# A two-pass channel-attention kernel: the first 26 rows of the second pass are loaded into the stream slots behind the last loads of the first

## The chip, the core and the metric

The kernel runs on one core of a Trainium2 chip. The metric is device time in microseconds (us) of one execution; the figure for a kernel is the median of its runs. TensorE is called PE in the profile's rows, VectorE DVE, ScalarE ACT, SyncE SP, GpSimd POOL. All loads and stores of the large tensor are issued by SP, in one order, onto one queue that 16 DMA engines work off.

## The reference

`x` has the shape (1, 384, 384, 384) in bfloat16, `w1d` holds one weight. The weight's window has length one, so the 1-D convolution over channels is a product:

```python
g  = jnp.einsum("bhwc->bc", x) / (H * W)      # mean over all 147456 positions
s  = sigmoid(g * w1d[0])
return x * s[:, None, None, :]
```

Every output element needs `s`, and `s` needs every input element. `x` is 113.25 MB; it does not fit into the core's on-chip memory, so a part of it has to be read twice.

## The kernel before, in words

**Rows.** The 147456 positions are 1152 rows for each of the 128 partitions. "A row" below is 128 partitions x 384 channels in bfloat16, which is 98304 bytes, and all buffers are counted in rows. One on-chip tensor, `arena` (L175), holds 275 of them; the names below are row numbers in it.

**Pass one** loads all 1152 rows, and PE adds each into `bank0` by a product with a matrix of ones (`sum_rows`, L224). Three kinds of rows pass through.

- *Streamed* rows (`stream`, L328): loaded, summed, overwritten. They are loaded again in pass two. There are `N_STREAM` = 785 of them.
- *Folded* rows (`fold`, L271): four rows are packed into the place of three by DVE and ACT, using exponent bits that are the same in the data; 296 rows are kept so, some of them in PSUM banks. They are unpacked in pass two by `unfold` (L446).
- *Raw* rows (`c_raw`, `N_RAW` = 71): the last 71 rows of pass one, which simply stay where they were loaded: 39 in area `A` (three slots of 13, L367, which streamed rows have used before), 8 each in `V`, `U`, `Y` and `T`. `U`, `V`, `Y` and `T` serve `fold` as scratch until then. `take_raw` (L414) writes their loads into the order: the three slots of `A`, then `V`, `U`, `Y`, `T` (5 and 3 rows).

**Between the passes** ACT computes the scale `s_bf` from `bank0` (L421). It waits for the last matmul; DVE's first multiplication waits for it; SP's first store waits for that.

**Pass two** multiplies each row by `s_bf` on DVE (`scale`, L428, whose instruction the profile has on L432) and stores it (`store`, L438, on L442). Rows that are free after their store are refilled with streamed rows, which are multiplied and stored in turn. Held and reloaded rows together make 1152 stores and 785 loads.

**What sets the order of pass two** is a planner that runs while the program is built (L539 to L717). It steps a clock from the moment the scale is there, keeps a list of what the queue has still to move (`moves`, with assumed costs per row and per transfer) and decides at each step what DVE does next (a multiplication from `landed`, or a piece of a folded pair), when a store is sent, and when a free run of rows is refilled (L695 to L706). What comes out is a fixed order of instructions on DVE and on SP. `Flow` (L21) adds the semaphore waits; SP takes its list strictly in order, so a load that waits for a store to land holds every transfer behind it.

The refill rule before is this:

```python
if n >= BIG or n == N_STREAM - todo or (ahead < LOW and n >= 8) or ahead < LAST:
```

Here `n` is the longest free run, `ahead` the planned backlog of the queue in us, `BIG` is 32 rows, `LOW` 9.0 and `LAST` 4.0.

Of the kernel before, what the change touches and what calls it, by code (L numbers as in the profile page):

```python
# [127 lines left out]
def kernel(  # L128
# [28 lines left out]
        areas.append((base, 3 * q))  # L157
        base += 3 * q
    RAW = {}
    for name, n in (("U", 8), ("V", 8), ("A", 39), ("Y", 8), ("T", 8)):  # L160
        RAW[name] = (base, n)
        base += n
    ROWS = base
    N_RAW = sum(n for _, n in RAW.values())
    U, V, A, Y, T = (RAW[n][0] for n in "UVAYT")

    BANKED = len(QS)
    PS = 3 * Q_BANKS
# [24 lines left out]
    def view(t, r0, n):  # L193
        return t[r0 * P : (r0 + n) * P, :].rearrange("(p r) c -> p r c", r=n)

    def rows(lo, n):
        return [("a", r) for r in range(lo, lo + n)]
# [3 lines left out]

    N_STREAM = RPP - N_RAW - sum(4 * q for q in QS)
    r = N_STREAM
    c_group = []
    for q in QS:
        c_group.append((r, 4 * q))
        r += 4 * q
    c_raw = (r, N_RAW)
    assert r + N_RAW == RPP

# [3 lines left out]
    def load(chunk, a, lo=0, hi=None):  # L214

        r0, n = chunk
        hi = n if hi is None else hi
        fl.add(
            "SP",
            lambda: nc.sync.dma_start(out=arena[:, a : a + hi - lo, :], in_=view(xf, r0, n)[:, lo:hi, :]),  # L220
            writes=rows(a, hi - lo), dma=True,
        )

    def sum_rows(a, n):  # L224
        def emit(i, first, last):
            return nc.tensor.matmul(acc, lhsT=ones[:], rhs=arena[:, i, :], start=first, stop=last)  # L226

        for i in range(a, a + n):
            first, last = summed[0] == 0, summed[0] == RPP - 1
            fl.add(  # L230
                "PE", lambda i=i, f=first, l=last: emit(i, f, l),
                reads=[("a", i), "ones"], writes=["bank0"],
            )
            summed[0] += 1
# [132 lines left out]
    SLOTS = [(A + i, 13) for i in range(0, 39, 13)]  # L367
# [3 lines left out]
    S1, S2, S3 = ([slot] for slot in SLOTS)  # L371
    B3, B4, AA = ([area] for area in (areas[3], areas[4], (A, 39)))

    def halves(area):
        a, n = area
        return [(a, n // 2), (a + n // 2, n - n // 2)]
# [4 lines left out]
        ([], B3), ([], B4),  # L381
        ([], B3), ([], AA),
        ([], halves(areas[4])), ([], S1 + S2 + S3),
        (S1, S2, S3 + S1), (S2, S3, S1 + S2 + S3),
    ]
    between = sum(n for b in BETWEEN[1:] for where in b for _, n in where)
    at = 0
    for g, q in enumerate(QS[:BANKED]):
        for lo in range(0, q, 2 * PIECE):
            n = min(2 * PIECE, q - lo)  # L390
# [19 lines left out]
            at += 1  # L410
    assert streamed[0] == N_STREAM

    def take_raw(a, n):
        load(c_raw, a, a - U, a - U + n)  # L414
        sum_rows(a, n)

    for a, n in SLOTS + [(V, 8), (U, 8), (Y, 8), (T, 5), (T + 5, 3)]:
        take_raw(a, n)
    assert summed[0] == RPP

    fl.add(  # L421
# [61 lines left out]
    def TT(n):  # L483
        return 0.15 + 0.2 * n
# [54 lines left out]
    ROW, PER_LOAD, PER_STORE = 0.2267, 0.112, 0.061  # L539
    LAT, SEEN, DT = 2.0, 1.5, 0.05  # L540
    PENDING, MERGE = 24.0, 12.0
    BIG, CAP, PART, LOW, LAST = 32, 48, 16, 9.0, 4.0
    BANKS_AT = 2
    now = dve_at = 0.0
    moves, waiting, over, acts = deque(), deque(), deque(), deque()
    landed = deque()
    idle = [False] * ROWS
    todo = 0
# [18 lines left out]
    def send(chunk, a, lo, hi, then, known=None):  # L567

        waiting.append((dve_at, hi - lo, then, chunk, a, lo, [] if known is None else known))

    def backlog():
        return sum(e[1] for e in moves) + ROW * sum(e[1] for e in waiting)

    def split(n, m):
        k = -(-n // m)
        cuts = [n * i // k for i in range(k + 1)]
        return list(zip(cuts, cuts[1:]))
# [12 lines left out]
        return f  # L590


    landed.append((c_raw, Y, Y - U, 4, False))
    landed.append((c_raw, Y + 4, Y - U + 4, 4, True))
    landed.append((c_raw, T, T - U, 8, True))
    landed.append((c_raw, U, 0, 8, True))
    for e, n in ((0, 8), (8, 13), (21, 13), (34, 13)):
        landed.append((c_raw, V + e, 8 + e, n, True))

    HALVES = (T, U)  # L600
    half = [True, True]
# [11 lines left out]
    def start_pair():  # L613

        nonlocal pair, bank_at
        if not line or needed or not half[pair % 2]:
            return False
        g, lo, n = line[0]
        if g == BANKED and (bank_at is None or now < bank_at[1]):
            return False  # L620
        line.popleft()
        h = pair % 2
        at = HALVES[h]
        half[h] = False
        pair += 1
        a = bank_at[0] if g == BANKED else areas[g][0]
        a += 3 * lo
        mine = [k for k in of_group(g) if lo <= pieces[k][1] < lo + n]

        def w_done():  # L630
            nonlocal out_rows
            out_rows += n
            release(a, 3 * n)

        def u_done():
            half[h] = True

        for k in mine:
            e = pieces[k][1] - lo
            fields, three, fourth = unfold(k, a + 3 * e, at + e)  # L640
            turns.extend((fields + (None,), three + (None,), fourth + (None,)))
        f, t, _ = turns[-2]
        turns[-2] = (f, t, lambda: send(c_group[g], a, 3 * lo, 3 * (lo + n), w_done, written))
        f, t, _ = turns[-1]
        turns[-1] = (f, t, lambda: send(c_group[g], at, 3 * QS[g] + lo, 3 * QS[g] + lo + n, u_done, written))
        return True

    while True:

        if dve_at <= now:  # L650
            ahead = backlog()
            can = bool(turns)
            if not can and (ahead >= PENDING or not landed):
                can = start_pair()
                if can and not asked:
                    verdict()
                    asked = True
            if landed and (ahead < PENDING or not can):
                chunk, a, lo, n, end = landed.popleft()
                scale(a, n)  # L660
                dve_at = now + TT(n)
                since = (a, lo) if since is None else since
                if end or ahead < MERGE:
                    b, first = since
                    send(chunk, b, first, lo + n, stored(b, lo + n - first))
                    since = None
            elif can:
                f, t, then = turns.popleft()
                f()
                dve_at = now + t  # L670
                if then:
                    then()
        while waiting and waiting[0][0] <= now:
            _, n, then, chunk, a, lo, known = waiting.popleft()
            known.append(store(chunk, a, lo, lo + n))
            moves.append([now + LAT, n * ROW + PER_STORE, then])
        if out_rows == total and not checked and all(half):
            checked = True
            fl.add("POOL", again, reads=["odd_i", "s_bf"], writes=rows(Y, N_OVER), after=written)
        while over and over[0][0] <= now:  # L680
            over.popleft()[1]()

        got = runs()
        if bank_at is None and len(line) <= len(QS) * 2 - BANKS_AT and got and max(got)[0] >= PS:
            a = max(got)[1]
            for i in range(a, a + PS):
                idle[i] = False
            back = arena[:, a : a + PS, :].rearrange("p r c -> p (r c)")
            for i, bk in enumerate(banks):
                lo, hi = i * BANK, min((i + 1) * BANK, PS * C)  # L690
                copy_bank(i, bk[:, 0 : hi - lo], back[:, lo:hi], [("bank", i)], rows(a, PS))
            bank_at = (a, now + 5.0)
            got = runs()

        if got and todo < N_STREAM:  # L695
            n, a = max(got)
            n = min(n, CAP, N_STREAM - todo)
            ahead = backlog()
            if n >= BIG or n == N_STREAM - todo or (ahead < LOW and n >= 8) or ahead < LAST:
                chunk = (todo, n)  # L700
                todo += n
                load(chunk, a)
                for i in range(a, a + n):
                    idle[i] = False
                parts = [(chunk, a + e, e, f - e, f == n) for e, f in split(n, PART)]
                moves.append([now + LAT, n * ROW + PER_LOAD, lambda parts=parts: landed.extend(parts)])  # L706

        if moves and moves[0][0] <= now:
            moves[0][1] -= DT
            if moves[0][1] <= 0:  # L710
                over.append((now + SEEN, moves.popleft()[2]))
        else:
            stall += DT
        if not (moves or waiting or over or landed or line or turns) and todo == N_STREAM:
            break
        now += DT
# [34 lines left out]
```

## Time and profile before

| | |
|---|---|
| median of 5 runs | 729.28 us (727.24 to 730.08) |
| the profiled execution, its time | 728.25 us |
| its span, first to last instruction | 726.5 us |
| DVE busy | 496.3 us (68%), 469 instructions |
| PE busy | 212.0 us (29%) |
| ACT busy | 115.4 us (16%) |
| bytes read from and written to HBM | 190.41 MB and 113.25 MB |
| mean rate over the span | 418 GB/s |

The profiled execution took 1.75 us more than its span, and is 1.03 us below the median of the runs. In the windows that are shown below, the columns after the busy time of each engine are the TensorE clock that was granted, the mean busy share of the 16 DMA engines, and the GB/s that they moved. Instructions on SP that issue transfers carry the line of `load` (L220) or of `store` (L442).

### The profile page before, as it was taken

What the parts mean: (1) busy time and instruction counts of PE and PEld (TensorE: products, weight loads), DVE (VectorE), ACT (ScalarE), POOL (GpSimd) and SP (SyncE); (2) the same over time, 40 slices, a digit from 0 to 9 for tenths busy, and PEclk for the clock granted to TensorE, in tenths of its full rate; (3) what the DMA queues carried; (4) which work ended last, traced back from release to release, by engine and by line L of the source; (5) the groups of instructions that cost most, each with busy time, mean ns of one, the idle gap of its engine ahead of it and who ended that gap; (6) DMA issues with size and microseconds to landing.
All of it is one profiled execution on the core that took longest, in us unless ns stands there. A gap on an engine that the chain in (4) does not pass through costs nothing.

```text
span 726.5 us, 3243 instructions
## 1 busy us (share of the span) xinstructions
PE 212.0 (29%) x1202; PEld 118.0 (16%) x1202; DVE 496.3 (68%) x469; ACT 115.4 (16%) x92; POOL 0.2 (0%) x4
## 2 busy tenths in 40 slices
PE   4677969889887770000000000000000000000000
PEld 2334535545443430000000000000000000000000
DVE  4600006987986729999989998999979994355340
ACT  3600004765764520000100000000000000000000
POOL 0000000000000000000000000000000000000000
PEclk9899999999999996555555555555555555555555
DMA  9999999999999978999999999999999999999996
GB/s 384 423 428 439 430 414 429 430 430 427 426 422 424 417 323 326 418 425 429 434 418 443 414 428 424 432 441 427 422 428 431 428 442 428 425 439 437 432 439 276
DMA packets 19890, 303.87 MB, mean 418 GB/s; under 512 B 2210, under 2 KB 2210, under 8 KB 6434
## 3 DMA queue, kind: packets, MB, share of 16 engines
q1 hardware_dynamic: 19872, 303.67, 98.5%
q8 instruction: 9, 0.15, 0.1%
q14 instruction: 7, 0.06, 0.0%
q10 hardware_dynamic: 2, 0.00, 0.0%
HBM read 190.41 MB, written 113.25 MB: 418 GB/s over the span
## 4 chain that ended last, share of the span: by engine, by line
DMA 58%; DVE 25%; PE 6%; another core or an unknown queue 4%; ACT 2%; SPq 1%; issue 0%; DVEq 0%
DMA arena<-in_x_dram 42%; DVE arena L432 17%; DMA out_dram<-arena 16%; PE bank L226 6%; DVE arena L250 5%; DVE arena L256 3%; ACT arena L290 2%; SPq L220 1%; ACT s_bf L423 0%; SPq L442 0%; PE bank L504 0%; DVE odd L499 0%; DVE odd_i L508 0%; DVE worst L494 0%
## 5 line engine op out<-in xcount | busy, mean ns | idle before, releaser
L432 DVE TENSOR_TENSOR arena<-arena,s_bf 128x1536 bf16<-128x1536 bf16 (+8 forms) x102 | 241.9, 2411 | 75.1 <-DMA arena<-in_x_dram 60.8
L250 DVE TENSOR_SCALAR arena<-arena 128x1536 uint16<-128x1536 uint16 (+2 forms) x247 | 145.8, 633 | 113.6 <-DMA arena<-in_x_dram 102.2
L226 PE MATMUL bank<-arena,ones 128*128 128x384 bf16 x1152 | 203.8, 338 | 57.7 <-DMA arena<-in_x_dram 57.7
L226 PEld LDWEIGHTS bank<-arena,ones 128*128 128x128 bf16 x1152 | 113.1, 101 | 148.1 <-DMA arena<-in_x_dram 63.7
L256 DVE TENSOR_TENSOR arena<-arena 128x1536 uint16<-128x1536 uint16 (+2 forms) x114 | 121.0, 1061 | 10.2 <-PE bank L226 8.1
L290 ACT ACTIVATE arena<-arena 128x3072 uint16<-128x3072 uint16 (+1 forms) x38 | 102.5, 2696 | 147.2 <-DVE arena L250 147.2
L360 ACT COPY arena<-bank 128x512 uint32<-128x512 uint32 (+1 forms) x7 | 4.0, 571 | 71.5 <-DMA out_dram<-arena 71.3
L241 PE MATMUL bank<-ones,zeros 128*128 128x384 bf16 x48 | 8.3, 326 | 0.0
L290 ACT ACTIVATION_READ_ACCUMULATOR arena<-arena 128x1 f32 x38 | 7.1, 187 | 0.0
L241 PEld LDWEIGHTS bank<-ones,zeros 128*128 128x128 bf16 x48 | 4.7, 98 | 3.1
L504 PE MATMUL bank<-odd,ones 128*128 128x1 bf16 x1 | 0.2, 187 | 15.8 <-DVE odd L499 15.8
L360 ACT COPY bank<-arena 128x512 uint32<-128x512 uint32 (+1 forms) x7 | 3.6, 567 | 0.0
L504 PEld LDWEIGHTS bank<-odd,ones 128*128 128x128 bf16 x1 | 0.1, 105 | 16.2 <-DVE odd L499 16.2
L423 ACT ACTIVATE s_bf<-bank,w_sc 128x384 bf16<-128x384 f32 x1 | 0.6, 581 | 12.9 <-PE bank L226 12.9
L719 ACT ACT_TABLE_LOAD x1 | 1.3, 1283 | 0.7 <-PEq L735 0.7
L320 DVE TENSOR_SCALAR w_sc<-bank 128x1 f32<-128x1 f32 x1 | 0.2, 157 | 1.1 <-PE bank L315 1.1
L310 DVE MEMSET ones<- 128x128 bf16 x1 | 0.2, 165 | 1.0 <-SPq L106 1.0
L315 PE MATMUL bank<-w_bf,ones 1*128 1x1 bf16 x1 | 0.2, 182 | 2.1 <-DMA w_bf<-in_w1d_dram 2.1
L315 PEld LDWEIGHTS bank<-w_bf,ones 1*128 1x128 bf16 x1 | 0.1, 100 | 2.1 <-DMA w_bf<-in_w1d_dram 2.1
L508 DVE CAST odd_i<-bank 128x1 int32<-128x1 f32 x1 | 0.2, 157 | 0.3 <-PE bank L504 0.3
L494 DVE TENSOR_REDUCE worst<-seen 128x1 f32<-128x38 f32 x1 | 0.2, 181 | 0.0
L499 DVE TENSOR_SCALAR odd<-worst 128x1 bf16<-128x1 f32 x1 | 0.2, 157 | 0.0
(5 smaller groups left out, 0.5 us busy)
## 6 DMA issues: line engine op xcount, KB each, us to landing
arena<-in_x_dram SPq DMA_DIRECT2D x17, 4608.0 KB, 34.7
out_dram<-arena SPq DMA_DIRECT2D x6, 4608.0 KB, 43.8
arena<-in_x_dram SPq DMA_DIRECT2D x21, 1248.0 KB, 12.0
arena<-in_x_dram SPq DMA_DIRECT2D x9, 2304.0 KB, 27.5
out_dram<-arena SPq DMA_DIRECT2D x8, 2304.0 KB, 28.9
arena<-in_x_dram SPq DMA_DIRECT2D x4, 4512.0 KB, 34.3
out_dram<-arena SPq DMA_DIRECT2D x3, 4512.0 KB, 26.8
out_dram<-arena SPq DMA_DIRECT2D x9, 1248.0 KB, 12.9
```

The costliest lines, as they stand in the source:

```text
L220: lambda: nc.sync.dma_start(out=arena[:, a : a + hi - lo, :], in_=view(xf, r0, n)[:, lo:hi, :]),
L226: return nc.tensor.matmul(acc, lhsT=ones[:], rhs=arena[:, i, :], start=first, stop=last)
L241: lambda: nc.tensor.matmul(acc, lhsT=zeros[:], rhs=ones[:, None, :].to_broadcast([P, C // P, P]), start=False, stop=False),
L250: lambda: nc.vector.tensor_scalar(out=dst, in0=src, scalar1=s0, scalar2=s1, op0=op0, op1=op1),
L256: "DVE", lambda: nc.vector.tensor_tensor(out=dst, in0=a, in1=b, op=op), reads=reads, writes=writes
L290: lambda: nc.scalar.activation(out=y, in_=y, func=ACTF.Copy, accum_out=seen[:, 2 * k + i : 2 * k + i + 1]),
L315: lambda: nc.tensor.matmul(votes, lhsT=ones[0:1, :], rhs=w_bf[0:1, 0:1], start=True, stop=True),
L360: "ACT", lambda: nc.scalar.copy(dst.bitcast(u32), src.bitcast(u32)), reads=reads, writes=writes
L423: lambda: nc.scalar.activation(out=s_bf[:], in_=acc, func=ACTF.Sigmoid, scale=w_sc[:, 0:1]),
L432: lambda: nc.vector.tensor_tensor(out=v, in0=v, in1=s_bf[:, None, :].to_broadcast([P, n, C]), op=Op.mult),
L504: lambda: nc.tensor.matmul(votes, lhsT=ones[:], rhs=odd[:], start=True, stop=True),
L719: nc.scalar.preload_act_table(ACTF.Sigmoid)
```

## The change

26 of the 39 rows of `A` no longer hold raw rows. Two slots of `A` (26 rows) take streamed rows once more at the end of pass one, so `N_RAW` goes from 71 to 45 and `N_STREAM` from 785 to 811. Behind the last load of pass one a load of the stream's first 26 rows is written into the order, into these two slots; it waits for PE to have summed the streamed rows in them. `HELD` is the third slot, which still holds 13 raw rows.

`A` is placed ahead of `U` in the arena, so that it lies beside the folded areas and the third slot beside `U`, and `V` lies between `U` and `Y`. The planner is told of the 26 rows as a transfer that is already under way (`AHEAD`). The rows it starts with are cut smaller (`V` in 4 and 4, `Y` and `T` in parts of 5, 5 and 6), and its refill rule asks for 12 free rows instead of 8 below a backlog of 9 us, and for 8 free rows instead of any below 4 us.

```diff
-    for name, n in (("U", 8), ("V", 8), ("A", 39), ("Y", 8), ("T", 8)):
+    for name, n in (("A", 39), ("U", 8), ("V", 8), ("Y", 8), ("T", 8)):
...
-    N_RAW = sum(n for _, n in RAW.values())
-    U, V, A, Y, T = (RAW[n][0] for n in "UVAYT")
+
+    N_AHEAD = 26
+    N_RAW = sum(n for _, n in RAW.values()) - N_AHEAD
+    A, U, V, Y, T = (RAW[n][0] for n in "AUVYT")
...
-        (S1, S2, S3 + S1), (S2, S3, S1 + S2 + S3),
+        (S1, S2, S3 + S1), (S2, S3, S1 + S2 + S3 + S1 + S2),
...
+    HELD = A + N_AHEAD
+
     def take_raw(a, n):
-        load(c_raw, a, a - U, a - U + n)
+        load(c_raw, a, a - HELD, a - HELD + n)
         sum_rows(a, n)
 
-    for a, n in SLOTS + [(V, 8), (U, 8), (Y, 8), (T, 5), (T + 5, 3)]:
+    for a, n in [(HELD, U - HELD), (V, 8), (U, 8), (Y, 8), (T, 5), (T + 5, 3)]:
         take_raw(a, n)
+
+    load((0, N_AHEAD), A)
...
+    AHEAD = N_AHEAD * ROW + PER_LOAD - 3.3
+    FIRST = 6
...
-    landed.append((c_raw, Y, Y - U, 4, False))
-    landed.append((c_raw, Y + 4, Y - U + 4, 4, True))
-    landed.append((c_raw, T, T - U, 8, True))
-    landed.append((c_raw, U, 0, 8, True))
-    for e, n in ((0, 8), (8, 13), (21, 13), (34, 13)):
-        landed.append((c_raw, V + e, 8 + e, n, True))
+    def parts(chunk, a):
+        n = chunk[1]
+        return [(chunk, a + e, e, f - e, f == n) for e, f in split(n, PART)]
+
+    for a, n, m in ((V, 8, 4), (Y, 16, FIRST), (U, 8, 8), (HELD, U - HELD, 8)):
+        for e, f in split(n, m):
+            landed.append((c_raw, a + e, a - HELD + e, f - e, f == n))
+    moves.append([0.0, AHEAD, lambda: landed.extend(parts((0, N_AHEAD), A))])
+    todo = N_AHEAD
...
-            if n >= BIG or n == N_STREAM - todo or (ahead < LOW and n >= 8) or ahead < LAST:
+            if n >= BIG or n == N_STREAM - todo or (ahead < LOW and n >= 12) or (ahead < LAST and n >= 8):
...
-                parts = [(chunk, a + e, e, f - e, f == n) for e, f in split(n, PART)]
-                moves.append([now + LAT, n * ROW + PER_LOAD, lambda parts=parts: landed.extend(parts)])
+                moves.append([now + LAT, n * ROW + PER_LOAD, lambda p=parts(chunk, a): landed.extend(p)])
```

## The prediction

> **What bounds the kernel now.** I read the page's slices first, then the windows in steps of 1 us around the join of the passes, the timeline there, the chain of waits, and last the order in which the changed program's instructions stand.
>
> ```profile
> DMA  9999999999999978999999999999999999999996
> GB/s 384 423 428 439 430 414 429 430 430 427 426 422 424 417 323 326 418 425 429 434 418 443 414 428 424 432 441 427 422 428 431 428 442 428 425 439 437 432 439 276
> ```
>
> The DMA engines are full in every slice but two in the middle and the last. DVE is busy 68%, and has idle stretches of 20 us after 600 us that delay nothing. So the time is bytes over rate, and whatever the engines are not moving. The window from 296 to 718 us has 430 GB/s, so one row of 98304 bytes costs 0.2286 us.
>
> ```profile
> 268.00:269.00 1.00, 0.57 (x4) 0.17 (x3) 0.00 (x0) 0.00 (x0) 0.00 (x0) 1.00 0.48 187
> 269.00:270.00 1.00, 1.00 (x7) 0.59 (x6) 0.00 (x0) 0.00 (x0) 0.00 (x0) 1.00 0.09 35
> 270.00:271.00 1.00, 1.00 (x9) 0.59 (x6) 0.00 (x0) 0.00 (x0) 0.00 (x0) 1.00 0.01 5
> ...
> 274.00:275.00 1.00, 0.00 (x0) 0.00 (x0) 1.00 (x2) 0.00 (x0) 0.00 (x0) 1.00 0.86 335
> 275.00:276.00 1.00, 0.00 (x0) 0.00 (x0) 1.00 (x2) 0.00 (x0) 0.00 (x0) 1.00 1.03 415
> 276.00:277.00 1.00, 0.00 (x0) 0.00 (x0) 1.00 (x1) 0.00 (x0) 0.00 (x0) 0.88 0.53 215
> ...
> 282.00:283.00 1.00, 0.00 (x0) 0.00 (x0) 1.00 (x1) 0.00 (x0) 0.00 (x0) 0.50 0.66 270
> ...
> 288.00:289.00 1.00, 0.00 (x0) 0.00 (x0) 1.00 (x3) 0.00 (x0) 0.00 (x0) 0.50 1.20 270
> 289.00:290.00 1.00, 0.00 (x0) 0.00 (x0) 1.00 (x2) 0.00 (x0) 0.00 (x0) 0.50 1.05 154
> ```
>
> The next-to-last column is the engines' busy share. After 268 they still work 0.48 + 0.09 + 0.01 = 0.58 us on average, the last of them until about 270.05; stores start at 274.14 (0.86 of that us). The gap is 5.56 us for the mean engine and 4.1 us for the slowest. Behind it lie small holes (0.47 us at 276, 0.34 us at 282), and a patch at 287 to 292 where the share is high but few bytes move: 1.83 us are lost there against 430 GB/s. In all, 274 to 298 has 375 GB/s, 24 x (1 - 375/430) = 3.07 us short.
>
> ```profile
> 268.88 2.77 PE L226 MATMUL bank<-arena,ones 128*128 128x384 bf16 x16 [0.43 <-DMA arena<-in_x_dram]
> 271.69 0.58 ACT L423 ACTIVATE s_bf<-bank,w_sc 128x384 bf16<-128x384 f32 x1 [12.93 <-PE bank L226]
> 272.30 5.16 DVE L432 TENSOR_TENSOR arena<-arena,s_bf 128x1536 bf16<-128x1536 bf16 x4 [13.64 <-ACT s_bf L423]
> 273.29 2.87 SPq L442 DMA_DIRECT2D out_dram<-arena  x3
> ```
>
> This is what the queue waits for in the gap: the last 16 matmuls, the sigmoid, the first multiplication, the first store's issue, and 0.85 us from its issue to its first byte.
>
> **The change, part by part.** *The load in the gap.* SP is through the last load of pass one at 260.09. The new load behind it waits for PE's sums of two slots; at their place in the trace of before these end at 262.48. So it is issued about 5.5 us before the queue runs dry, and its 26 rows, 26 x 0.2286 = 5.94 us, follow without a hole. They fill the gap of 5.56 us.
>
> *What they replace.* The gap is filled with work that before did not exist. Pass one still loads 1152 rows. Pass two stored 1152 and loaded 785, 1937 rows; now 811, of which 26 lie in the gap, so the same 1937 remain behind it. Filling the gap is paid for in full by the 26 rows no longer held: +5.94 - 5.56 = +0.38 us for the mean engine, +5.94 - 4.1 = +1.84 us for the slowest. This is the main result: the title's saving is a wash by bytes.
>
> *The holes behind the gap.* Before, the queue lived from hand to mouth: each store was issued as soon as DVE had multiplied its rows. Now it has work until about -3.70 + 5.94 = 2.24 us after the scale is ready (272.28), and the first store can start at 0.95 + 0.05 + 0.85 = 1.85. The chain has 71 rows in eight multiplications in 14.84 us; from the 13-row group (2.77 us) and the 4-row group (0.96) a row is 0.20 us and an instruction about 0.09. The first five stores (24 rows) are then multiplied at 5.2 us and can start at 6.1, and the queue gets to the fifth at 6.4. Both holes close: -0.81 us.
>
> *DVE.* It gets three more multiplications in 102 and no more rows, 0.3 us, in time that it has idle late. The dangerous place is the first store of 24 unfolded rows, for which SP waits while loads stand behind it. In the changed order 270 rows are queued ahead of it: -3.70 + 270 x 0.2286 = 58.0 us after the scale. DVE needs by then 79 raw and reloaded rows in eleven multiplications (16.8), the check of the folding (0.73, from 287.14 to 287.87), three pieces of 16 rows but the last four rows (a piece is 1.41 + 0.88 + 0.56 + 0.87 + 1.27 + 0.87 + 2.47 + 0.48 + 0.96 = 9.8 in the chain; 27.9), and 51 rows more (10.9): 56.3, and 57.2 with issue. The spare is 0.8 us, so I take 0. If DVE waits there for a late load, the queue stands by as much: bound +1.5.
>
> *Waits that move on SP.* The load now ahead of the first reload's place, 8 rows into `V`, stands behind five stores and waits for the first two to land. They end at 2.24 + 8 x 0.2286 = 4.1; the 384 KB stores of before took 2.5 us from issue to landing, about 1.5 us of that beyond the transfer, so it is free at 5.6, and SP is there at 5.5. It holds nothing. The other reloads stand 3 us or more behind their stores.
>
> *More and smaller transfers.* Pass two had 26 loads and 56 stores; the changed order has 30 and 61, nine more. Before, 12- and 13-row loads (202 to 248 us) moved 423 GB/s and 48-row ones (53 to 107 us) 431. Over 46 us that is 0.86 us for some 12 more transfers, 0.07 each: +0.63.
> The Trainium skill's page "DMA: Bandwidth & Descriptors" (Rules for kernel authors) wants 1 MiB per transfer or more, and its fit under Anatomy of one DMA has 2.0 us fixed for each; the change's first eight stores are 384 to 768 KB, and nine transfers that each paid this would make +18 us. That fit is for another issuing path, and the two 384 KB stores at 275 us, at 415 GB/s, do not show it; I go by the rows.
>
> *The last loads of pass one, with 26 rows behind them.* `U`, `Y` reach PE at 266.97 and 268.88, one load's pace apart with the queue full. At that pace the last 3 rows land at 268.88 + 8 x 0.2286 = 270.7, and PE turns to them at 268.88 + 13 x 0.173 = 271.1. With 0.4 us to spare I take 0; bound +0.4.
> The same page (Latency and other measured facts) gives HBM access as 0.2 us on average and 2 us at high load, which speaks against the change, since these rows would now land under load; by it the scale would come up to 1.8 us later. The trace's pace of 1.91 us between two full-queue landings shows no such step.
>
> *The patch at 287 to 292.* Nothing in the profile names its cause; it begins with the first reload behind 14 us of pure stores. The changed order puts the first reload behind 24 rows of stores. I leave it in: 0, bounds -1.83 and 0.
>
> **Sum.** Mean engine: +0.38 - 0.81 + 0.63 = +0.20. Slowest engine: +1.84 - 0.81 + 0.63 = +1.66. The end is the last engine's: after 718 us the share falls over six us, 0.74, 0.45, 0.45, 0.36, 0.26, 0.13. But the engine that was late in pass one need not be the late one of pass two, so I take the middle, +0.9 us: 728.25 + 0.9 = 729.15 for an execution like the profiled one. That one was 1.03 us below the median, so I forecast 730.2.
>
> **The rivals.** *Slower: the lag is no longer reset (0.29).* All engines started pass two together after the gap. Without a pause an engine 2 us late stays late, and a load or store counts as landed only when its last engine is done, so reloads and slots come later too. For it: the two tails above, 2 and 6 us long. Against it: in the planned order a load is queued several us before DVE needs it. Price: +1.66, and up to the pass-one lag of 2 us once more where SP waits for a 24-row store: up to +3.7, of which what is over 2.2 counts here, 731.5 to 733.0. It decides once the tail after the bulk of the transfers grows by over a microsecond.
>
> *Faster: the early loss goes whole (0.15).* If the patch belongs to the pure stores, the 3.07 us vanish: +0.38 + 0.63 - 3.07 = -2.1, and with fewer waits of DVE for reloads (6.2 us in 274 to 420 us) up to -3.5: 725.8 to 727.2. Against it: a part of it is no hole, but slow transfers.
>
> *The load is not in the gap (0.03).* If SP is held until the last sums, the 26 rows start at about 272.5 and stand ahead of the first store, which then starts at 273.35 + 5.94 = 279.3 instead of 274.14: +5.15 - 0.81 + 0.63 = +5.0, 734.3.
>
> *No measurable change (0.53):* the sum, 727.1 to 731.4. About 0.3%, 2.2 us, is what a measurement of this kernel can tell from no change.
>
> **Range.** 726.5 to 733.5: it takes in the bounds (-1.83; +0.4, +1.5) about the sum and most of both rivals. Chances: faster by over 0.3% 0.15, within 0.53, slower 0.32 (0.29 + 0.03).
>
> **What would show it.** Right: near 100% DMA share from 268 to 298 us; HBM read 192.97 MB instead of 190.41; the first multiplication within 0.5 us of 272.3; the span between 725 and 729. The bytes step is wrong if fewer bytes are read or pass two's 1937 rows end earlier from the same start. The lag rival shows in a longer tail at the end, the DVE step in SP waiting for DVE ahead of a 24-row store, the faster rival in 430 GB/s from 274 to 298.

## The result: 0.23% slower, a wash by bytes with a small loss

The changed kernel's median is 730.62 us (29 runs, 728.36 to 734.5) against 728.76 us before (50 runs, 727.24 to 731.13). The ratio is 1.0023, with a 95% interval of 1.0014 to 1.0031: +1.7 us, +1.0 to +2.3. That is inside the 0.3% that were set as "no measurable change" and above the +0.9 us of the sum. The forecast of 730.2 us stood on five runs of the kernel before with a median of 729.28; with 50 runs it is 728.76. That 730.2 lies so near to 730.62 is therefore partly luck: the base was 0.5 us too high, and the change was put about 0.8 us too low.

The profiled execution of the changed kernel took 727.12 us, with a span of 725.3 us. It is 3.5 us below its own median and faster than the profiled one of before (728.25). So its rows can show how the join of the passes looks, but not the 1.7 us.

The slices of its page, and the page's line on bytes:

```profile
DMA  9999999999999999999999999999999999999997
GB/s 380 430 423 442 429 418 425 431 431 426 426 422 422 413 415 374 427 398 428 427 427 443 416 432 424 437 414 426 447 424 435 418 448 424 437 434 429 437 432 329
HBM read 192.97 MB, written 113.25 MB: 422 GB/s over the span
```

The two weak slices in the middle are gone, and 2.56 MB more are read, the 26 rows. The windows in steps of 1 us at the same places as before (the last two columns are the DMA engines' busy share and GB/s):

```profile
268.00:269.00 1.00, 0.58 (x4) 0.21 (x3) 0.00 (x0) 0.00 (x0) 0.00 (x0) 1.00 1.29 528
269.00:270.00 1.00, 1.00 (x9) 0.60 (x7) 0.00 (x0) 0.00 (x0) 0.00 (x0) 1.00 1.04 437
270.00:271.00 1.00, 1.00 (x8) 0.61 (x7) 0.00 (x0) 0.00 (x0) 0.00 (x0) 1.00 1.07 462
...
272.00:273.00 1.00, 0.00 (x0) 0.00 (x0) 0.91 (x2) 0.06 (x1) 0.00 (x0) 1.00 0.93 399
...
276.00:277.00 1.00, 0.00 (x0) 0.00 (x0) 1.00 (x2) 0.00 (x0) 0.00 (x0) 0.50 1.04 416
...
280.00:281.00 1.00, 0.00 (x0) 0.00 (x0) 1.00 (x2) 0.00 (x0) 0.00 (x0) 0.50 1.51 312
281.00:282.00 1.00, 0.00 (x0) 0.00 (x0) 1.00 (x2) 0.00 (x0) 0.00 (x0) 0.50 0.84 181
282.00:283.00 1.00, 0.00 (x0) 0.00 (x0) 1.00 (x1) 0.00 (x0) 0.00 (x0) 0.50 0.71 154
283.00:284.00 1.00, 0.00 (x0) 0.00 (x0) 1.00 (x1) 0.00 (x0) 0.00 (x0) 0.50 0.82 295
```

The gap is full, and so is the hole at 276. The patch in which the engines are busy and few bytes move is still there; it has moved from 287 to 280 and costs the same: 4 - (312 + 181 + 154 + 295) / 430 = 1.8 us, as the 1.83 before. The timeline of the join shows that the scale does not come later with a load running behind the last rows:

```profile
268.67 2.77 PE L228 MATMUL bank<-arena,ones 128*128 128x384 bf16 x16 [0.42 <-DMA arena<-in_x_dram]
271.48 0.58 ACT L429 ACTIVATE s_bf<-bank,w_sc 128x384 bf16<-128x384 f32 x1 [12.25 <-PE bank L228]
...
278.42 0.34 SPq L222 DMA_DIRECT2D arena<-in_x_dram  x1
```

The sigmoid is at 271.48, 0.2 us earlier than before. The last line is the first reload of pass two; the patch begins 1.6 us after its issue, as it began two to three us after that at 284.87 in the kernel before.

The end of the span, first of the changed kernel, then of the kernel before (windows of both):

```profile
719.00:720.00 1.00, 0.00 (x0) 0.00 (x0) 0.00 (x0) 0.00 (x0) 0.00 (x0) 0.50 1.07 461
720.00:721.00 1.00, 0.00 (x0) 0.00 (x0) 0.00 (x0) 0.00 (x0) 0.00 (x0) 0.50 0.43 184
721.00:722.00 1.00, 0.00 (x0) 0.00 (x0) 0.00 (x0) 0.00 (x0) 0.00 (x0) 0.50 0.60 258
722.00:723.00 1.00, 0.00 (x0) 0.00 (x0) 0.00 (x0) 0.00 (x0) 0.00 (x0) 0.50 0.22 92
```

```profile
719.00:720.00 1.00, 0.00 (x0) 0.00 (x0) 0.00 (x0) 0.00 (x0) 0.00 (x0) 0.50 0.45 194
720.00:721.00 1.00, 0.00 (x0) 0.00 (x0) 0.00 (x0) 0.00 (x0) 0.00 (x0) 0.50 0.45 194
721.00:722.00 1.00, 0.00 (x0) 0.00 (x0) 0.00 (x0) 0.00 (x0) 0.00 (x0) 0.50 0.36 152
722.00:723.00 1.00, 0.00 (x0) 0.00 (x0) 0.00 (x0) 0.00 (x0) 0.00 (x0) 0.50 0.26 111
723.00:724.00 1.00, 0.00 (x0) 0.00 (x0) 0.00 (x0) 0.00 (x0) 0.00 (x0) 0.50 0.13 55
```

Adding up the shares, the engines stop on average at 720 + 0.43 + 0.60 + 0.22 = 721.25 in the changed kernel, and at 718 + 0.74 + 0.45 + 0.45 + 0.36 + 0.26 + 0.13 = 720.39 before: the mean engine ends 0.86 us later. The last engine ends about 1 us earlier in this one execution. The time of an execution is the last engine's, which is why one profile of each does not settle a fifth of a per cent.

### The profile page after: what moved, and what is told of

The parts are those of the page before. It is cut to its first block, busy times and chain, and to the rows that moved or that the text cites. A ratio compares the mean times of both kernels' runs of the same rounds, so it can differ in the third digit from the quotient of the medians.

```text
span 725.3 us, 3255 instructions
## 1 busy us (share of the span) xinstructions
PE 215.0 (30%) x1202; PEld 119.3 (16%) x1202; DVE 496.7 (68%) x472; ACT 115.4 (16%) x92; POOL 0.2 (0%) x4
## 3 DMA queue, kind: packets, MB, share of 16 engines
HBM read 192.97 MB, written 113.25 MB: 422 GB/s over the span
## 4 chain that ended last, share of the span: by engine, by line
DMA 66%; DVE 20%; PE 6%; ACT 2%; SPq 1%; issue 0%; DVEq 0%
DMA arena<-in_x_dram 43%; DMA out_dram<-arena 24%; DVE arena L438 13%; PE bank L228 6%; DVE arena L252 4%; DVE arena L258 3%; ACT arena L292 2%; SPq L222 1%; ACT s_bf L429 0%; SPq L448 0%; PE bank L510 0%; DVE odd L505 0%; DVE worst L500 0%; DVEq L112 0%; DVE odd_i L514 0%
## 5 line engine op out<-in xcount | busy, mean ns | idle before, releaser
L228 PE MATMUL bank<-arena,ones 128*128 128x384 bf16 x1152 | 206.8, 341 | 54.5 <-DMA arena<-in_x_dram 54.4
```

## The experiments

My theory, from the prediction: the change is a wash by bytes, and what is left over comes from DMA engines that no longer start pass two together (the lag). Rivals: the new order of stores and reloads costs by itself, or only the mean engine counts. All ratios are against the kernel before on the same chip.

### First set: the change taken apart

**order_only**: no row ahead, everything else of the change.

```diff
-    N_AHEAD = 26
+    N_AHEAD = 0
...
-        (S1, S2, S3 + S1), (S2, S3, S1 + S2 + S3 + S1 + S2),
+        (S1, S2, S3 + S1), (S2, S3, S1 + S2 + S3),
...
-    for a, n in [(HELD, U - HELD), (V, 8), (U, 8), (Y, 8), (T, 5), (T + 5, 3)]:
+    for a, n in SLOTS + [(V, 8), (U, 8), (Y, 8), (T, 5), (T + 5, 3)]:
...
-    load((0, N_AHEAD), A)
...
-    for a, n, m in ((V, 8, 4), (Y, 16, FIRST), (U, 8, 8), (HELD, U - HELD, 8)):
+    for a, n, m in ((V, 8, 4), (Y, 16, FIRST), (U, 8, 8), (HELD, U - HELD, 13)):
...
-    moves.append([0.0, AHEAD, lambda: landed.extend(parts((0, N_AHEAD), A))])
```

> The changed program with no row loaded ahead: the new places in the arena, the smaller first parts and the new refill rule alone. 71 raw rows and 785 reloads as before, but 29 loads and 67 stores in pass two against 26 and 56, and the gap between the passes stays empty. By bytes: 14 more transfers at 0.07 us, and nothing else, +1.0 us (+0.3 to +1.4). If the cost of the change (+1.7 us) lies in the engines' lag that is not reset, this kernel, which resets it, shows only those transfers. If the cost lies in the new order of stores and reloads, it shows +1.7 us or more.

Measured: 1.0003 (0.9992 to 1.0013), 728.7 us. The new order costs nothing that can be seen; the interval is about 0.8 us wide to either side. Its profile has the hole at 276 closed without any load ahead:

```profile
276.00:277.00 1.00, 0.00 (x0) 0.00 (x0) 1.00 (x2) 0.00 (x0) 0.00 (x0) 0.76 1.01 405
```

The stretch from 274 to 298 us has 389 GB/s against 375, which is 0.8 us won, and that would pay for its 14 transfers: 14 x 0.07 - 0.81 = +0.2 us. The +1.0 us that was expected had left the holes out.

**ahead_only**: the kernel before with the load ahead alone.

```diff
-    N_RAW = sum(n for _, n in RAW.values())
+    N_AHEAD = 26
+    N_RAW = sum(n for _, n in RAW.values()) - N_AHEAD
...
-        (S1, S2, S3 + S1), (S2, S3, S1 + S2 + S3),
+        (S1, S2, S3 + S1), (S2, S3, S1 + S2 + S3 + S1 + S2),
...
+    def lo_of(a):
+        return a - U - (N_AHEAD if a >= A else 0)
...
-    for a, n in SLOTS + [(V, 8), (U, 8), (Y, 8), (T, 5), (T + 5, 3)]:
+    for a, n in SLOTS[2:] + [(V, 8), (U, 8), (Y, 8), (T, 5), (T + 5, 3)]:
         take_raw(a, n)
+    load((0, N_AHEAD), A)
...
-    for e, n in ((0, 8), (8, 13), (21, 13), (34, 13)):
-        landed.append((c_raw, V + e, 8 + e, n, True))
+    for a, n in ((V, 8), (A + N_AHEAD, 13)):
+        landed.append((c_raw, a, lo_of(a), n, True))
+    moves.append([0.0, N_AHEAD * ROW + PER_LOAD - 3.3, lambda: landed.extend(((0, N_AHEAD), A + e, e, 13, e == 13) for e in (0, 13))])
+    todo = N_AHEAD
```

> The kernel before with the 26 rows loaded ahead and 45 raw rows, but with the old places in the arena, the old first parts and the old refill rule. 29 later or earlier loads (811 rows) and 59 stores, six transfers more than before. By bytes, for the mean engine: +0.38 - 0.81 + 0.42 = 0.0 us; with the lag of the slowest engine +1.5 us. If the new order is what costs, this kernel is level with the one before (within 0.5 us).

Measured: 1.0030 (1.0017 to 1.0044), +2.2 us. In this order the cost came with the load ahead; its size is near what the lag gives.

**late**: the rows held are those of the change, but the load stands behind the first two stores.

```diff
-    load((0, N_AHEAD), A)
...
-    moves.append([0.0, AHEAD, lambda: landed.extend(parts((0, N_AHEAD), A))])
+    def late():
+        load((0, N_AHEAD), A)
+        moves.append([now + LAT, N_AHEAD * ROW + PER_LOAD, lambda: landed.extend(parts((0, N_AHEAD), A))])
+
+    over.append((3.0, late))
     todo = N_AHEAD
```

> The changed program, with the load of 26 rows not ahead of the first store but behind the first two. Rows held and rows reloaded are those of the change (45 and 811). By bytes the gap is empty again and the 26 rows cost their full price: +5.94 us and six transfers more, +6.4 us against before (+5.3 to +7), some 4.5 us above the change. If the transfers were not the limit, or the load behind the first stores were hidden, it would be within 1 us of the change.

Measured: 1.0097 (1.0083 to 1.0112), 735.81 us, +7.1 us. Its windows at the join (the first store's bytes come in the 273 window):

```profile
271.00:272.00 1.00, 0.36 (x3) 0.00 (x0) 0.00 (x0) 0.58 (x1) 0.00 (x0) 1.00 0.00 0
272.00:273.00 1.00, 0.00 (x0) 0.00 (x0) 0.99 (x2) 0.00 (x0) 0.00 (x0) 1.00 0.00 0
273.00:274.00 1.00, 0.00 (x0) 0.00 (x0) 1.00 (x2) 0.00 (x0) 0.00 (x0) 1.00 0.18 71
...
282.00:283.00 1.00, 0.00 (x0) 0.00 (x0) 0.00 (x0) 0.00 (x0) 0.00 (x0) 0.50 0.77 240
283.00:284.00 1.00, 0.00 (x0) 0.00 (x0) 0.00 (x0) 0.00 (x0) 0.00 (x0) 0.50 0.64 257
```

The gap is empty again and the 26 rows cost 5.94 us or more. The +7.1 us lies just above the +5.3 to +7 that were expected: DVE (the third busy column) has run out of rows at 282, and the queue stands for 0.6 us. This is the heart of the matter: the load ahead does bring some 5 us (7.1 - 1.7 = 5.4, of which some 0.6 may be this hole), and giving up 26 held rows takes them away.

**ahead13**: half the load.

```diff
-    N_AHEAD = 26
+    N_AHEAD = 13
...
-        (S1, S2, S3 + S1), (S2, S3, S1 + S2 + S3 + S1 + S2),
+        (S1, S2, S3 + S1), (S2, S3, S1 + S2 + S3 + S1),
...
-    for a, n in [(HELD, U - HELD), (V, 8), (U, 8), (Y, 8), (T, 5), (T + 5, 3)]:
+    for a, n in [(HELD, 13), (HELD + 13, 13), (V, 8), (U, 8), (Y, 8), (T, 5), (T + 5, 3)]:
...
-    AHEAD = N_AHEAD * ROW + PER_LOAD - 3.3
+    AHEAD = max(0.05, N_AHEAD * ROW + PER_LOAD - 3.3)
...
-    for a, n, m in ((V, 8, 4), (Y, 16, FIRST), (U, 8, 8), (HELD, U - HELD, 8)):
+    for a, n, m in ((V, 8, 4), (Y, 16, FIRST), (U, 8, 8), (HELD, U - HELD, 13)):
```

> The changed program with 13 rows ahead in place of 26: 58 raw rows, 798 reloads. 13 rows are 2.97 us, so a pause of 2.6 us is left for the mean engine and of about 1.1 us for the slowest: all engines start pass two together. By bytes again a wash: 2.97 us of work for 2.97 us of gap; 13 transfers more, +0.9 us. If the lag costs, it is level with the kernel without a row ahead; if the load ahead costs by itself, it lies half-way between that one and the change.

Measured: 1.0003 (0.9994 to 1.0012), 728.86 us. Its windows show the pause that is left:

```profile
271.00:272.00 1.00, 0.52 (x4) 0.10 (x1) 0.00 (x0) 0.45 (x1) 0.00 (x0) 1.00 0.41 170
272.00:273.00 1.00, 0.00 (x0) 0.00 (x0) 0.83 (x1) 0.14 (x1) 0.00 (x0) 1.00 0.07 30
273.00:274.00 1.00, 0.00 (x0) 0.00 (x0) 1.00 (x3) 0.00 (x0) 0.00 (x0) 1.00 0.01 3
274.00:275.00 1.00, 0.00 (x0) 0.00 (x0) 1.00 (x2) 0.00 (x0) 0.00 (x0) 1.00 1.03 402
```

The last engine is done before 274, and all start the stores together. With 0 and with 13 rows the bytes cancel to within about 0.1%; in this order the loss appears between 13 and 26.

### Second set: how full the gap may be

**ahead24**:

```diff
-    N_AHEAD = 26
+    N_AHEAD = 24
...
-        (S1, S2, S3 + S1), (S2, S3, S1 + S2 + S3 + S1 + S2),
+        (S1, S2, S3 + S1), (S2, S3, S1 + S2 + S3 + S1 + [(A + 13, 11)]),
...
-    for a, n in [(HELD, U - HELD), (V, 8), (U, 8), (Y, 8), (T, 5), (T + 5, 3)]:
+    for a, n in [(HELD, 2), (HELD + 2, 13), (V, 8), (U, 8), (Y, 8), (T, 5), (T + 5, 3)]:
```

> 24 rows ahead in place of 26: 5.49 us of work in a gap that is 5.56 us for the mean engine and 4.1 us for the slowest. If only the mean engine counted, the gap is not overfilled and the kernel is level with the ones with 0 and 13 rows ahead (ratio 1.000, within 0.001). If the slowest engine sets the end, 1.4 us of its lag are carried over: +1.2 us or more, ratio 1.0015 to 1.003, close to the change.

Measured: 1.0019 (1.0005 to 1.0032). It is on the lag's side; the interval shuts out 1.000 narrowly.

**ahead39**:

```diff
-    N_AHEAD = 26
+    N_AHEAD = 39
...
-        (S1, S2, S3 + S1), (S2, S3, S1 + S2 + S3 + S1 + S2),
+        (S1, S2, S3 + S1), (S2, S3, S1 + S2 + S3 + S1 + S2 + S3),
...
-    for a, n in [(HELD, U - HELD), (V, 8), (U, 8), (Y, 8), (T, 5), (T + 5, 3)]:
+    for a, n in [(V, 8), (U, 8), (Y, 8), (T, 5), (T + 5, 3)]:
...
-    AHEAD = N_AHEAD * ROW + PER_LOAD - 3.3
+    AHEAD = max(0.05, N_AHEAD * ROW + PER_LOAD - 3.3)
...
-    for a, n, m in ((V, 8, 4), (Y, 16, FIRST), (U, 8, 8), (HELD, U - HELD, 8)):
+    for a, n, m in ((V, 8, 4), (Y, 16, FIRST), (U, 8, 8)):
```

> All 39 rows of the area ahead, no raw row in it: 8.92 us of work for the same gap. Mean engine alone: +3.36 us beyond the gap, holes -0.81, six transfers more +0.4: +2.9 us, ratio 1.004. With the lag that the change shows (+1.7 to +2.2 us with 26 rows) and 13 rows more at 2.97 us: +4.7 to +5.2 us, ratio 1.0065 to 1.007. If overfilling were free, as it would be if DVE and not the transfers set pass two, it stays at the change's 1.002.

Measured: 1.0043 (1.0030 to 1.0055), +3.1 us, the figure of the mean engine and not of the lag. But its profile lacks the slow patch behind the first reload, so the 1.8 us that both figures had left in did not occur. With that taken off, the lag's +4.7 to +5.2 us becomes +2.9 to +3.4, and the mean engine's +2.9 becomes +1.1. By its number the run is on the mean engine's side, and by its profile, which is one execution, on the lag's; I take it as deciding nothing between the two. It does show that rows beyond the gap are paid for.

**after_again**, the changed kernel once more:

> The changed kernel once more, beside the others on the same chip: 1.0014 to 1.0031 as in its first runs, with a wider spread of its times than the kernel before (6.1 us against 3.9 us). If the first result were an accident of the chip, it moves to 1.000.

Measured: 1.0012 (1.0001 to 1.0024), 728.9 us, 727.43 to 731.02. Slower again, by less than expected (+0.9 us), and with a spread of 3.6 us: the wider spread of the first runs did not come back.

**short_gap**: the kernel before, with a shorter chain in the gap.

```diff
-    for a, n in SLOTS + [(V, 8), (U, 8), (Y, 8), (T, 5), (T + 5, 3)]:
+    for a, n in SLOTS + [(V, 8), (U, 8), (Y, 4), (Y + 4, 4), (T, 5), (T + 5, 3)]:
...
-    landed.append((c_raw, Y, Y - U, 4, False))
+    landed.append((c_raw, Y, Y - U, 2, True))
+    landed.append((c_raw, Y + 2, Y + 2 - U, 2, True))
```

> The kernel before, nothing loaded ahead, with the chain in the gap cut: Y is loaded in two parts of 4 rows, so that PE can begin on it 0.9 us earlier, and the first part that DVE multiplies and SP stores is 2 rows instead of 4 (0.4 us earlier). Two transfers more, +0.14 us. If the gap is idle time of the queue that counts in full, and bytes alone set the rest: -0.5 to -1.2 us, ratio 0.9985 to 0.9993. If the last 3 rows land too late for PE to finish earlier, only the 0.4 us remain: 0.9996, which is not seen.

Measured: 1.0009 (0.9998 to 1.0021): no gain. Its timeline says why:

```profile
267.10 2.77 PE L226 MATMUL bank<-arena,ones 128*128 128x384 bf16 x16 [0.20 <-DMA arena<-in_x_dram]
270.18 1.47 PE L226 MATMUL bank<-arena,ones 128*128 128x384 bf16 x8 [0.30 <-DMA arena<-in_x_dram]
271.69 0.58 ACT L423 ACTIVATE s_bf<-bank,w_sc 128x384 bf16<-128x384 f32 x1 [12.90 <-PE bank L226]
```

PE is done with `Y` early, and then waits until 270.18 for the last 8 rows; the sigmoid is at 271.69 as before. The mean engine has stopped at 268.6 (shares of 0.49, 0.09 and 0.02 in the three us from 268); the last of the 16, still at work after 270, makes these rows land. The lag at the end of pass one is part of the gap itself.

### Third set: another refill rule, and a pause put back

**order13**, **ahead13_13** and **after13** are order_only, ahead13 and the changed kernel, each with one more edit:

```diff
-            if n >= BIG or n == N_STREAM - todo or (ahead < LOW and n >= 12) or (ahead < LAST and n >= 8):
+            if n >= BIG or n == N_STREAM - todo or (ahead < LOW and n >= 12) or (ahead < LAST and n >= 12):
```

> No row ahead, as in order_only, but no refill below 12 rows: the early reload of 8 rows into V goes, and the first reload is three times 13 rows behind 71 rows of stores, as in ahead39, whose profile has no slow patch. 91 transfers in pass two against 82. If the 8-row reload among the first stores makes the patch: holes -0.81, transfers +0.63, patch -1.5: -1.7 us, ratio 0.9977 (0.997 to 0.9985). If every first reload behind stores has its patch, it stays level, 1.000.

Measured: 1.0020 (1.0011 to 1.0030). The forecast gain became a loss of 1.5 us. Windows of order13:

```profile
282.00:283.00 1.00, 0.00 (x0) 0.00 (x0) 1.00 (x2) 0.00 (x0) 0.00 (x0) 0.50 0.37 149
...
291.00:292.00 1.00, 0.00 (x0) 0.00 (x0) 1.00 (x3) 0.00 (x0) 0.00 (x0) 0.50 1.10 290
292.00:293.00 1.00, 0.00 (x0) 0.00 (x0) 1.00 (x1) 0.00 (x0) 0.00 (x0) 0.50 0.78 200
```

The patch is there, now behind the first reload of 13 rows (issued at 287.81), and without the early reload the queue runs dry at 282 for 0.63 us. So the 8-row reload is not the patch's cause, and it feeds the queue. The loss itself is not explained by this: order13 is ahead of the kernel before from 274 to 298 (384 against 375 GB/s, 0.5 us won) and behind it from 298 to 340 (418 against 425, 0.7 us lost). So an order of stores and loads can cost 1.5 us with the gap left empty, and what order_only showed holds for its own order alone.

> 13 rows ahead and no refill below 12 rows. 92 transfers. By bytes level with order13, since a pause for all engines is left: 0.9977 if the patch goes with the 8-row reload, 1.000 if not.

Measured: 1.0023 (1.0015 to 1.0032), level with order13, as by bytes, and like it above both values that were expected.

> The changed kernel (26 rows ahead) and no refill below 12 rows. Against ahead13_13 it has the full gap, so the lag of the slowest engine is carried: +1.4 us more than ahead13_13, whatever the patch does. If the mean engine alone counted it lies 0.3 us above ahead13_13.

Measured: 1.0019 (1.0008 to 1.0029), level with ahead13_13 where +1.4 us more were expected. With 26 rows the hole at 282 is filled (share 0.99), which is worth 0.6 us, so the lag had +0.8 us to show; the difference is -0.3 us, and the two intervals are about 0.7 us wide to either side. In this order the full gap costs nothing that can be seen: here the lag as a cost fails.

**reset**: the changed kernel, its first store held until the 26 rows have landed.

```diff
     load((0, N_AHEAD), A)
+    gate = [fl.steps[-1]]
...
-            reads=rows(a, hi - lo), dma=True,
+            reads=rows(a, hi - lo), dma=True, after=[gate.pop()] if gate else (),
```

> The changed kernel with one more wait: the first store is held until the 26 rows have landed, so all engines start the stores together again, at about 277.1 us (last engine's end 276.0, wake-up 0.2, issue to first byte 0.85) against 274.14 before. If the late engine sets the end, only its own pause counts, 277.1 against its 276.2: +0.9 us over the change, 1.0032 to 1.004 against before, with the narrow spread of before. If the lag costs nothing and the mean engine counts, its pause is 277.1 - 274.4 = 2.7 us: 1.0055 to 1.006.

```profile
275.00:276.00 1.00, 0.00 (x0) 0.00 (x0) 1.00 (x2) 0.00 (x0) 0.00 (x0) 0.50 0.10 40
276.00:277.00 1.00, 0.00 (x0) 0.00 (x0) 1.00 (x2) 0.00 (x0) 0.00 (x0) 0.50 0.00 0
277.00:278.00 1.00, 0.00 (x0) 0.00 (x0) 1.00 (x2) 0.00 (x0) 0.00 (x0) 0.50 0.40 154
```

```profile
276.77 3.52 SPq L449 DMA_DIRECT2D out_dram<-arena  x5
```

The pause is there, with the first store issued at 276.77 and its bytes from 277.6, half a microsecond later than expected: no run shows the 0.2 us that was put for the wake-up, and here some 0.8 us pass from the last engine's end at about 276.0 to the issue. Measured: 1.0042 (1.0028 to 1.0056), +3.1 us against before and +1.4 to +2.2 over the two measurements of the change. It lies between what the two theories said (1.0032 to 1.004, and 1.0055 to 1.006). The pause as it came is 277.6 - 276.0 = 1.6 us for the late engine and 277.6 - 274.6 = 3.0 us for the mean one (shares of 0.52 and 0.10 from 274), so the result is nearer the lag's, with an interval of 1 us to either side. Six runs between 730.64 and 733.65 do not show a narrower spread.

## Why the prediction was right

**The load in the gap: right.** It runs without a hole, and the scale is not later (the sigmoid is at 271.48 against 271.69), so the bound of +0.4 us for a later scale came to nothing. The Trainium skill's figure for HBM access at high load, 2 us ("DMA: Bandwidth & Descriptors", Latency and other measured facts), does not show here either.

**The wash by bytes: right, and shown.** 192.97 MB were read as forecast. late (+7.1 us), order_only and ahead13 (both +0.2 us) give the three points: the rows' price without the gap, none, and half of each. The traces show it more closely. They keep 16 landing marks for each transfer, as many as there are DMA engines, and I take each mark for one engine. The mean of the 16 marks of the last store is at 721.1 us before, 720.9 in order_only, 720.6 in ahead13, 721.2 in ahead_only, 727.3 in late, and 722.0 and 721.0 in the two profiled executions of the change. So the mean engine ends within 0.9 us of the kernel before in all of these but late, and 6.2 us later in late. (ahead24, at 722.6 in its one profile, is 1.5 us later.)

**The holes: right in kind, a little large.** 274 to 298 us has 385 GB/s against 375, so 24 x 10 / 430 = 0.56 us came back instead of 0.81. One reading in this step was loose: the 13-row and the 4-row group alone give about 0.16 us for an instruction and not 0.09. The whole chain bears the 0.09 out: the change's first eleven multiplications, 79 rows, took 16.64 us, for 79 x 0.20 + 11 x 0.09 = 16.8.

**The first reload's wait on SP: right that it holds nothing, too short.** It was to be free 5.6 us after the scale; it was issued at 278.42, some 6.4 us after. SP waited for the second store to land: the mean of that store's marks is at 277.38, the last at 278.41. The queue had stores to work off meanwhile.

**The transfers: not contradicted.** 14 more of them and the closed holes came out at +0.2 us in order_only, for +0.17 from 0.07 us each; with 0.8 us to either side this does not measure the 0.07, but 2.0 us for each, the fixed cost of the fit that the prediction cites, would have made +28 us and is out.

**The patch: right to leave it in.** It moved with the first reload and kept its 1.8 us. The faster rival, for which it had to vanish, is out.

**The last engine: the term that was sized by a choice.** The sum stood at +0.20 us for the mean engine and +1.66 for the slowest, and I took +0.9, the middle. The first measurement gave +1.7 (1.0 to 2.3), the second +0.9 (0.1 to 1.7). That more than the mean engine counts is supported by ahead24, ahead_only and, weakly, by reset; after13 speaks against a lag that always costs, and order13 shows as large a loss without one. The sign named for it, a longer tail at the end, is not in the profiled execution.

The landing marks show which part of the mechanism is true. In the kernel before, the 16 marks of the last load of pass one lie 2.3 us apart and those of the first store 0.2 us. In the change it is 1.7 us for the load and 1.7 for the first store. So the pause does bring the engines into step, and without it the lag is carried into pass two: that part is shown. But at the last store the marks lie 5.8 us apart before and 3.2 in the change: the engines drift apart again within pass two, and the kernel before, which started it from 0.2 us, ends further apart than the change. The last mark of that store comes 1.8 to 5.7 us after the mean one in the six profiles that carried the lag, and 3.5 to 5.4 in the eight that did not. That the carried lag is what the change costs is therefore not shown, and where its last microsecond goes is not settled: it appears when the gap is filled to the brim, in two orders of three. The slower rival as it was put, 731.5 to 733.0, did not occur.

**DVE at the first 24-row store: right.** The mean share of the DMA engines from 296 to 716 us is 1.01 in both profiles, so nothing stood there. The rate was 429 GB/s in the change and 430 before, which is 1 us in that execution; in its second profile, after_again, it was 430 again from 298 to 716.

## What to carry to other kernels

In a kernel that is bound by its transfers, first count bytes on both sides of the gap: a buffer that is given up so that an idle stretch can be filled costs as much as it brings, row for row, until the stretch is full, and more beyond. Here filling only half of it was free; so was not filling it. An idle stretch that all transfer engines share is also the place where they fall into step again (marks 2.3 us apart ahead of it, 0.2 behind it), and the last engine, not the mean one, decides when data have landed and when the kernel ends. That being out of step at the start of a stage costs time at its end is another matter: over 450 us the engines here drifted further apart than they had been at its start.

## What was not expected of the hardware

- The first reload behind the first stores is followed by two to four microseconds at 120 to 370 GB/s with the engines busy, some 1 to 3 us after its issue, in every profile of this study but that of ahead39 (issues at 284.87, 278.42 and 287.81 us in before, the change and order13; slow from 287, 280 and 291). Why ahead39 is spared, with its first reload issued at 290.30, was not found.
- By the landing marks the 16 DMA engines end pass two over 3.2 to 8.4 us in the 14 profiles, and pass one over 1.4 to 2.5 us. Which engine is the last one, and why the lag grows, was not found.
- One execution with a profile lay 3.5 us below the median of its kernel: its last mark came 1.8 us after the mean one, against 4.5 us in the second profile of the same kernel. At this size of effect a profile tells where, not how much.
